# A list schedule that follows TensorE's column quarters, and a closing product on 128 rows

## The chip, the cores and the metric

The kernel runs on one core of a Trainium2 chip. The metric is device microseconds (us) of one execution, taken over several runs. The core's engines each take their instructions strictly in the order in which the program has them: PE (TensorE, matrix products into the accumulators of PSUM), DVE (VectorE), ACT (ScalarE), POOL (GpSimd), and SP, which here only issues DMAs. An engine whose next instruction must wait for another engine keeps everything behind it waiting too.

## The reference, cut to what matters

A recurrent attention over 768 steps, for 4 batches of 8 heads with 40 channels, and behind it two dense stages:

```python
for t in range(S):
    y[:, :, t] = np.einsum('bhd,bhde->bhe', rt, state)
    Sa = np.einsum('bhde,bhe->bhd', state, at)
    state_decay = state * wt[:, :, None, :] - np.einsum('bhd,bhe->bhde', Sa, bt)
    state = state_decay + np.einsum('bhd,bhe->bhde', vt, kt)
...
a = x @ w1
b = x @ w2
h = a * b @ w3
x = h @ w_out
...
h = x @ w_in
g = h * np.cos(h)
return g @ w_out
```

x has 3072 tokens of 320 channels; w1 and w2 are 320 x 1024, w_in is 320 x 2048.

## The kernel before

The 768 steps are cut into 24 chunks of 32 steps. All 32 pairs of batch and head go through a chunk together, as 16 pairs in two halves (hf 0 and 1). For each chunk the recurrence is turned into small dense products in fp32. In the order in which a chunk needs them they are called, by the functions that write them: **g** (`gstage`, 64x144, the chunk's own matrices), **mv** (32x64), **z** (40x64), **q** (32x72), **u** (32x72, on 32 rows), **y** (40x72) and **s** (40x40, the state for the next chunk). Each writes to a part of PSUM's partitions: a product with 32 output rows occupies one of TensorE's four column quarters, one with 40 or 64 rows two of them, one with 128 rows all four. In the profile every fp32 product is two records, so 16 products of y are "x32"; where the kernel's order is listed, it is one.

The products of four chunks (a group) need one triangular inverse, `tinv`, which DVE and POOL work out elementwise (dozens of operations on each). It ends with a transpose on DVE, `tfin`, which u of the group's first chunk waits for. There are six groups.

When two chunks are done, their output, 256 tokens, is one slab, and there are 12. `slab` loads it (`load_x`), `split_x` splits it into a high part `xh` (ACT) and a low part (POOL), each number being held as the sum of two of the faster format fp32r, and `ab` multiplies it by w1 and w2: eight steps f, and in each, for w1 and for w2, a sum of eight products 128x256. The third block of 64 channels lies twice in the 128 rows of `xh[:, 2]`, and the weight block `R` holds the high part of the weights in rows 0 to 63 and their low part in rows 64 to 127; so one product of 128 rows covers two terms. The eighth product, the sum's closing one, has the 64 rows `R[H0]` against `xr`, the low part of the third block. Each sum is then copied and multiplied (ACT, DVE) and stored (`pd`). `fold34` multiplies w3 by w_out beforehand (six products 128x320 for each of 32 units, "f,f" in the profile), `convert` and `weights_c` unpack weights on DVE, ACT and POOL.

After the last chunk come the second dense stage's products for all 12 slabs (`x2`, `hh`, `oo`: 3456 products, all in fp32r).

What sets the order: the kernel's functions do not issue instructions. They record them in `Program`, and its `emit` (line 256) orders them by a list schedule: it keeps a clock for each engine and always lets the engine that is free first take, among the instructions whose inputs are there, the one with the longest chain of work behind it (`far`). The lengths come from `length` and from tables (COST, HOP between engines, STEP of a product). A product's length is scaled by the share of columns that it occupies, as if narrow products always ran side by side. When PE's next product is of another form (32 rows or more, fp32 or fp32r: `mode`), SWITCH is added, unless a sum that has been started can go on. All instructions are issued at line 318, so the profile's rows are told apart by the tiles that they write and read: xs is the slab's split input (xh, xl, xr), w among the ab rows its weights, X and r the chunk's matrices, mid small work tiles, sh the tiles of g and of the inverse.

Of the kernel before, what the change touches and what calls it, by code (L numbers as in the profile page):

```python
# [10 lines left out]
F32 = mybir.dt.float32  # L11
F32R = mybir.dt.float32r
I32 = mybir.dt.int32
ALU = mybir.AluOpType
# [12 lines left out]
T2 = 256  # L27
# [102 lines left out]
class Program:  # L130
# [104 lines left out]
    def length(self, n):  # L235
# [16 lines left out]
    def mode(self, n):  # L252
        kw = self.calls[n][3]
        return kw["lhsT"].ap[0][1] <= 32, kw["rhs"].dtype

    def emit(self, tc, nc):
        self.link()
        N = len(self.calls)
        eng = [c[0] for c in self.calls]
        cost = [self.length(n) for n in range(N)]  # L260
        after = [[] for _ in range(N)]
        for n, d in enumerate(self.deps):
            for j in d:
                after[j].append(n)
        far = [0.0] * N
        hop = lambda n, m: self.HOP[eng[n]] if eng[m] != eng[n] else self.OWN[eng[n]]
        for n in reversed(range(N)):
            x = cost[n][1] + (self.ISSUE + self.BEGIN + self.END if eng[n] == "sync" else 0)
            far[n] = x + max([far[m] + hop(n, m) for m in after[n]], default=0)
# [6 lines left out]
        lanes, moved = deque([0.0] * self.LANES), 0.0  # L276
# [3 lines left out]
        for k in range(N):  # L280
# [4 lines left out]
            n = heapq.heappop(ready[e])[1]  # L285
            if e == "tensor":
# [1039 lines left out]
```

## Time and profile before

| what | us |
|---|---|
| runs | 1219.82, 1231.59, 1233.6 (median 1231.59) |
| the profiled execution, a run of its own | 1221.59 |
| its span, first to last instruction | 1219.8 |

The mean granted clock of TensorE was 0.944 in the profiled execution. Its parts, marked by the inverse's transposes and the last y: up to 108 us the first group is prepared; to 712 us run the 24 chunks, with most of the ab products between; to 808 us the last ab products, the last weights and the start of the second dense stage; to the end that stage alone.

A row of a timeline reads: start in us, length in us, engine, operation, tiles out<-in, rows*columns of the product, shape of the moving operand, and how many records follow each other. The length runs to the end of the last record, and ends of products are modelled; so what a piece of work takes from PE is read from its start to the start of the next row. A row of the groups has busy time, mean ns of one, and the engine's idle time before them. A row of the waits has the engine that waits, the one waited for, us in total, times, and the longest.

### The profile page before, as it was taken

The page shows a single profiled execution, that of the slowest core. Times are in us where ns is not written, and L with a number is a line of the kernel's source. Part 1 is how long each engine was busy: PE and PEld are TensorE (multiplying, and loading weights), DVE is VectorE, ACT ScalarE, POOL GpSimd, SP SyncE. Part 2 cuts the span into 40 slices and gives each one's busy share as a digit, 9 for nine tenths or more (in the row PEclk, how much of TensorE's full clock was granted, in tenths as well). Part 3 has the DMA queues.
Part 4 walks back from the last instruction along what each step waited for, and adds up shares of the span by engine and source line. Part 5 has one row for each costly group of instructions (what it writes and reads, how often), then busy time and mean ns, then how long its engine had stood idle before and what let it go on. Part 6 is the DMA issues. An engine that isn't in the chain of part 4 may idle for free. (4 is left out here: it accounts for less than half of the span.)

```text
span 1219.8 us, 34120 instructions
## 1 busy us (share of the span) xinstructions
PE 1052.4 (86%) x13536; PEld 956.4 (78%) x13536; DVE 842.2 (69%) x1776; ACT 679.3 (56%) x1750; POOL 600.4 (49%) x734
## 2 busy tenths in 40 slices
PE   2434798869987998999889977999999999999997
PEld 1324687768776877878778865899999999999997
DVE  9797779668968887896796674785455554545444
ACT  5865545754676578478545542455455544555443
POOL 8666336435444533563566673463455443454222
PEclk9975799889988999999899987999999999999999
DMA  6643544443454445444446553411101111011000
GB/s 177 185 117 93 140 119 123 126 137 115 129 157 131 114 141 158 127 134 114 137 136 209 150 169 106 124 39 47 46 12 46 44 38 46 22 37 46 9 4 23
DMA packets 142128, 122.73 MB, mean 101 GB/s; under 512 B 68240, under 2 KB 114832, under 8 KB 140432
## 3 DMA queue, kind: packets, MB, share of 16 engines
q1 hardware_dynamic: 141824, 120.50, 34.4%
q8 instruction: 106, 1.74, 0.6%
q14 instruction: 54, 0.44, 0.1%
q10 hardware_dynamic: 144, 0.06, 0.0%
HBM read 86.95 MB, written 29.62 MB: 96 GB/s over the span
## 5 line engine op out<-in xcount | busy, mean ns | idle before, releaser
L318 PE MATMUL bank<-xs,w 128*128 128x256 f32 (+1 forms) x1536 | 281.3, 316 | 29.9 <-ACT xs L318 22.0
L318 PEld LDWEIGHTS bank<-xs,w 128*128 128x128 f32 (+1 forms) x1536 | 221.3, 200 | 75.2 <-ACT xs L318 23.8
L318 POOL TENSOR_TENSOR w<-w,w 128x512 fp32r<-128x512 f32 x96 | 127.9, 1333 | 237.5 <-ACT w L318 147.4
L318 POOL TENSOR_SCALAR_AFFINE_SELECT X<-X 32x256 f32<-32x256 f32 (+1 forms) x144 | 98.6, 685 | 113.2 <-ACT X L318 92.1
L318 ACT COPY mid<-bank 128x256 f32<-128x256 f32 (+2 forms) x190 | 71.7, 394 | 144.9 <-PE bank L318 138.3
L318 ACT COPY X<-bank 32x128 f32<-32x128 f32 (+1 forms) x384 | 124.3, 324 | 41.8 <-PE bank L318 36.3
L318 DVE SCALAR_TENSOR_TENSOR w<-w,bank 128x512 f32<-128x512 int32 x96 | 65.8, 687 | 117.6 <-ACT w L318 106.0
L318 ACT COPY r<-bank 64x160 f32<-64x160 f32 (+2 forms) x408 | 113.4, 281 | 43.7 <-PE bank L318 38.7
L318 PE MATMUL bank<-X,r 104*40 104x72 f32 (+3 forms) x3072 | 124.2, 238 | 12.8 <-POOL X L318 7.1
L318 DVE TENSOR_TENSOR X<-bank,mid 40x128 f32<-40x128 f32 (+1 forms) x276 | 97.9, 355 | 51.0 <-PE bank L318 46.0
L318 PE MATMUL bank<-xs,r 128*128 128x256 f32 x576 | 130.5, 282 | 0.5 <-DVE xs L318 0.5
L318 PE MATMUL bank<-D,r 128*128 128x256 f32 x576 | 129.2, 282 | 1.8 <-DVE w L318 1.7
L318 PEld LDWEIGHTS bank<-X,r 104*40 104x40 f32 (+3 forms) x3072 | 104.5, 118 | 25.1 <-POOL X L318 8.6
L318 ACT CAST w<-w 128x512 fp32r<-128x512 f32 x120 | 73.6, 620 | 85.5 <-PE bank L318 70.5
L318 PE MATMUL bank<-mid 32*32 32x72 f32 (+2 forms) x3040 | 92.6, 233 | 26.6 <-ACT r L318 18.6
L318 PE MATMUL bank<-r,w 128*128 128x320 f32 x432 | 107.7, 311 | 0.6 <-ACT r L318 0.6
L318 PEld LDWEIGHTS bank<-mid 32*32 32x32 f32 (+2 forms) x3040 | 72.2, 126 | 42.7 <-ACT r L318 20.3
L318 PEld LDWEIGHTS bank<-D,r 128*128 128x128 f32 x576 | 99.2, 189 | 2.5 <-DVE w L318 2.2
L318 PEld LDWEIGHTS bank<-xs,r 128*128 128x128 f32 x576 | 99.9, 189 | 0.7 <-DVE xs L318 0.7
L318 DVE TENSOR_TENSOR sh<-sh,sh 128x110 f32<-128x110 f32 (+6 forms) x216 | 85.1, 394 | 2.4
L318 DVE SCALAR_TENSOR_TENSOR w<-w 128x512 f32<-128x512 int32 x96 | 84.6, 882 | 1.9
L318 PE MATMUL bank<-more,w 128*128 128x320 f32 x360 | 84.9, 310 | 0.0
(92 smaller groups left out, 2278.9 us busy)
## 6 DMA issues: line engine op xcount, KB each, us to landing
pd<-mid SPq DMA_DIRECT2D x96, 128.0 KB
f<-w3t SPq DMA_DIRECT2D x32, 256.0 KB
sh<-kb SPq DMA_DIRECT2D x48, 160.0 KB
sh<-wa SPq DMA_DIRECT2D x96, 80.0 KB
X<-pd SPq DMA_DIRECT2D x6, 1024.0 KB
w<-pd SPq DMA_DIRECT2D x6, 1024.0 KB
w34d<-f SPq DMA_DIRECT2D x32, 160.0 KB
r<-wo SPq DMA_DIRECT2D x16, 320.0 KB
```

The costliest lines, as they stand in the source:

```text
L318: getattr(getattr(nc, e), method)(*args, **kw)
```

## The change

Two things. First, the closing product of each ab sum has 128 rows: `split_x` makes a low part of all three blocks in one POOL operation of 128x768, in place of one of 128x512 and one of 64x256, and the sum ends with `R` against `xh[:, 2]` and `R` against `xl[:, 2]`. (The second of these adds the product of both low parts, which was left out.) No product with 64 rows is left.

Second, the list schedule. It keeps a time for each of the four column quarters (`array`); a product starts when its own quarters are free, and a product of another form when all are, plus SWITCH. If the first choice would have to wait for its quarters, `beside` takes another ready product of the same form whose quarters are free. `mode` tells 64 rows apart too. A sum that has been started still goes on ahead of a product of another form. HOP, and the lengths of DVE's and POOL's tensor_tensor and of DMAs, are longer, SWITCH shorter. The drawn variations (`rng`) are not used, since RUNS is 0.

```diff
-    STEP, DEEP = {True: 1.67, False: 0.457}, {True: 180, False: 185}
+    STEP, DEEP = {True: 1.67, False: 0.457}, 185
...
-        ("scalar", "copy"): (205, 0.72), ("scalar", "activation"): (200, 0.9), ("vector", "tensor_tensor"): (155, 1.1),
+        ("scalar", "copy"): (205, 0.72), ("scalar", "activation"): (200, 0.9), ("vector", "tensor_tensor"): (165, 1.25),
...
-        ("gpsimd", "tensor_tensor"): (330, 2.05), ("gpsimd", "affine_select"): (250, 1.2), ("gpsimd", "memset"): (110, 0.82),
+        ("gpsimd", "tensor_tensor"): (380, 2.3), ("gpsimd", "affine_select"): (250, 1.2), ("gpsimd", "memset"): (110, 0.82),
...
-    HOP = {"tensor": 95, "scalar": 65, "vector": 70, "gpsimd": 40, "sync": 60}
-    ISSUE, GAP, BEGIN, RATE, END, STORE, LANES, SWITCH, WAIT = 350, 55, 1350, 380, 1100, 600, 8, 120, 100
+    HOP = {"tensor": 140, "scalar": 110, "vector": 120, "gpsimd": 90, "sync": 60}
+    ISSUE, GAP, BEGIN, RATE, END, STORE, LANES, SWITCH, WAIT = 370, 60, 1350, 380, 1600, 600, 8, 90, 100
+    RUNS, LATE, VARY = 0, 500, {"vector": (0.9, 1.25), "gpsimd": (0.9, 1.4), "scalar": (0.95, 1.1)}
...
         if k == "matmul":
-            a = kw["rhs"]
-            w = min(x for x in (32, 64, 128) if x >= size(kw["lhsT"]))
-            step = 4 + self.STEP[a.dtype == F32] * size(a) * w / 128
-            return step, self.DEEP[a.dtype == F32] + step * 128 / w / 2 if a.dtype == F32 else self.DEEP[False] + step
+            f = kw["rhs"].dtype == F32
+            step = 2 + self.STEP[f] * size(kw["rhs"])
+            return step, self.DEEP + step / (2 if f else 1)
...
     def mode(self, n):
+
         kw = self.calls[n][3]
-        return kw["lhsT"].ap[0][1] <= 32, kw["rhs"].dtype
-
-    def emit(self, tc, nc):
-        self.link()
+        return kw["lhsT"].ap[0][1] <= 32, kw["lhsT"].ap[0][1] <= 64, kw["rhs"].dtype
+
+    def columns(self, n):
+
+        out = self.aps[n][0][0]
+        r = out.offset // math.prod(out.tensor.shape[1:])
+        return range(r // 32, (r + out.ap[0][1] + 31) // 32)
+
+    def beside(self, n, t, mode, array, ready, far):
+
+        if self.kinds[n] == mode and max(array[i] for i in self.quarters[n]) > t + 20:
+            x = min((x for x in ready if self.kinds[x[1]] == mode and max(array[i] for i in self.quarters[x[1]]) <= t + 5), default=None)
+            if x:
+                ready.remove(x)
+                ready.append((-far[n], n))
+                heapq.heapify(ready)
+                return x[1]
+        return n
+
...
-        lanes, moved = deque([0.0] * self.LANES), 0.0
+        lanes, moved, array = deque([0.0] * self.LANES), 0.0, [0.0] * 4
...
+            step, whole = cost[n]
             if e == "tensor":
-                if more is not None and not left[more] and self.mode(n) != mode and when[more] <= t + self.WAIT:
-                    if n != more:
-                        heapq.heappush(ready[e], (-far[n], n))
-                        n = more
-                        ready[e].remove((-far[n], n)) if (-far[n], n) in ready[e] else later[e].remove((when[n], n))
-                        heapq.heapify(ready[e])
-                        heapq.heapify(later[e])
-                        t = max(t, when[n])
+                if more is not None and more != n and not left[more] and self.kinds[n] != mode and when[more] <= t + self.WAIT:
+                    heapq.heappush(ready[e], (-far[n], n))
+                    n = more
+                    x = (-far[n], n)
+                    (ready if x in ready[e] else later)[e].remove(x if x in ready[e] else (when[n], n))
+                    heapq.heapify(ready[e])
+                    heapq.heapify(later[e])
+                    t = max(t, when[n])
+                    step, whole = cost[n]
+                else:
+                    n = self.beside(n, t, mode, array, ready[e], far)
+                    step, whole = cost[n]
                 more = self.sums.get(n)
-            step, whole = cost[n]
-            _, method, args, kw = self.calls[n]
-            if method == "matmul":
-                if self.mode(n) != mode:
-                    t += self.SWITCH
-                mode = self.mode(n)
-            if method == "dma_start":
+                if self.kinds[n] != mode:
+                    t = max(t, *array) + self.SWITCH
+                mode = self.kinds[n]
+                t = max(t, *(array[i] for i in self.quarters[n]))
+                for i in self.quarters[n]:
+                    array[i] = t + step
+                step = max(13, min(array) - t)
+            elif e == "sync":
                 t = max(t, lanes.popleft())
                 moved = max(moved, t + step + self.BEGIN) + whole
-                whole = moved + self.END + self.STORE * (kw["out"].space == DRAM) - t
+                whole = moved + self.END + self.STORE * (self.calls[n][3]["out"].space == DRAM) - t
+                if rng:
+                    whole += rng.expovariate(1 / self.LATE)
                 lanes.append(t + whole)
                 step += self.GAP
-            start[n] = (t, k)
+            elif rng:
...
+        runs = [self.run(far, cost, after, random.Random(k)) for k in range(self.RUNS)]
+        mean = self.run([-sum(x) for x in zip(*runs)] if runs else far, cost, after, None)
         with tc.manual_schedule():
-            for n in sorted(range(N), key=lambda n: start[n]):
+            for n in self.sorted(mean, after):
                 e, method, args, kw = self.calls[n]
                 getattr(getattr(nc, e), method)(*args, **kw)
+
...
-        xh, xl, xr = self.xh, self.xl, self.xr
+        xh, xl = self.xh, self.xl
         nc.scalar.copy(xh, xf)
-        nc.gpsimd.tensor_tensor(out=xl, in0=xf[:, 0:2], in1=xh[:, 0:2].bitcast(F32), op=ALU.subtract)
-        nc.gpsimd.tensor_tensor(out=xr, in0=xf[H0, 2], in1=xh[H0, 2].bitcast(F32), op=ALU.subtract)
-        return xh, xl, xr
+        nc.gpsimd.tensor_tensor(out=xl, in0=xf, in1=xh.bitcast(F32), op=ALU.subtract)
+        return xh, xl
...
-        xh, xl, xr = x
+        xh, xl = x
...
-            ops += [(R[:, w, fs], xh[:, 2])] + [(T[i][0][:, w, fs], xl[:, i]) for i in range(2)] + [(R[H0, w, fs], xr)]
+            ops += [(T[i][0][:, w, fs], xl[:, i]) for i in range(2)] + [(R[:, w, fs], xh[:, 2]), (R[:, w, fs], xl[:, 2])]
             for n, (l_, r_) in enumerate(ops):
                 nc.tensor.matmul(P[:, w], lhsT=l_, rhs=r_, start=(n == 0), stop=(n == len(ops) - 1))
...
-        self.xh, self.xl, self.xr = t(128, 3, T2), t(128, 2, T2), t(64, T2)
+        self.xh, self.xl = t(128, 3, T2), t(128, 3, T2)```

What moves, at two places. The first is PE in chunk 12, the first of the fourth group, from its first y product to its last ones before the next chunk. Names: X with r is y where it says 40x72, sh is g, r with X is s, mid 32x72 is u, xs is ab, and f with f is fold34. Before:

```order
L318 MATMUL bank<-X,r_77 40x72 x8
L318 MATMUL bank<-sh_63 64x144 x8
L318 MATMUL bank<-r_77,X 40x40 x16
L318 MATMUL bank<-mid 32x72 x16
L318 MATMUL bank<-X,r_77 40x72 x8
L318 MATMUL bank<-f_81,f_94 128x320
L318 MATMUL bank<-xs,w_88 128x256
L318 MATMUL bank<-f_81,f_94 128x320
```

The same place now:

```order
L357 MATMUL bank<-r_77,X 40x40 x16
L357 MATMUL bank<-X,r_77 40x72 x16
L357 MATMUL bank<-xs,w_88 128x256 x2
L357 MATMUL bank<-xs,w_90 128x256 x4
L357 MATMUL bank<-xs,w_88 128x256
L357 MATMUL bank<-xs,w_90 128x256 x3
L357 MATMUL bank<-sh_63 64x144 x8
L357 MATMUL bank<-mid 32x72 x16
```

The first half's 16 y products stood as two pieces of eight, each in one half of the columns, with g, s and u between; now they stand together, both halves by turns. Over the whole program, 228 of the y products followed one in the same columns directly; now it is 54. For q it is 76 and now 7, for s 27 and now 67. PE goes from fp32 into a stretch of fp32r products 158 times before and 136 times now; of the 192 closing products, 113 stood before an fp32 product, 57 inside a stretch ahead of a 128-row product, and 22 ahead of another closing one. Between fp32 products of different forms the order changes 118 times before, 141 times now. What stands in each chunk is otherwise nearly as it was: of the ab products, 168 stood behind the last y, now 180; ahead of y of chunk 12 stand 768 in both.

The second place is POOL around the split of the eleventh slab (xs<-mid,xs), with the recurrence's masks (AFFINE_SELECT on X) and the unpacking of weights (r, f, sh). Before:

```order
L318 TENSOR_TENSOR r_78<-r_73,r_78 128x256 x2
L318 AFFINE_SELECT X<-X 32x8x32 x2
L318 TENSOR_TENSOR xs<-mid,xs 128x512
L318 TENSOR_TENSOR xs<-mid,xs 64x256
L318 TENSOR_TENSOR f_95<-sh_64,f_95 128x640
L318 TENSOR_TENSOR r_78<-r_73,r_78 128x320
```

Now:

```order
L357 TENSOR_TENSOR r_78<-r_73,r_78 128x256
L357 AFFINE_SELECT X<-X 32x8x32 x2
L357 TENSOR_TENSOR r_78<-r_73,r_78 128x256
L357 TENSOR_TENSOR xs<-mid,xs 128x768
L357 TENSOR_TENSOR f_95<-sh_64,f_95 128x640
L357 AFFINE_SELECT X<-X 32x8x32
```

Two operations have become one, and its neighbours have changed places.

More of the change, by code (lines that the diff above doesn't have):

```diff
@@ L2 @@
 import math
+import random
 from collections import deque
@@ L253, in mode, with run @@
         kw = self.calls[n][3]
-        return kw["lhsT"].ap[0][1] <= 32, kw["rhs"].dtype
-    def emit(self, tc, nc):
-        self.link()
-        N = len(self.calls)
[L259 to L265, printed above, removed]
+        return kw["lhsT"].ap[0][1] <= 32, kw["lhsT"].ap[0][1] <= 64, kw["rhs"].dtype
[12 more added lines that the diff above has]
+        return n
+    def run(self, far, cost, after, rng):
+        N = len(self.calls)
+        eng = self.eng
         hop = lambda n, m: self.HOP[eng[n]] if eng[m] != eng[n] else self.OWN[eng[n]]
-        for n in reversed(range(N)):
-            x = cost[n][1] + (self.ISSUE + self.BEGIN + self.END if eng[n] == "sync" else 0)
-            far[n] = x + max([far[m] + hop(n, m) for m in after[n]], default=0)
         left = [len(d) for d in self.deps]
@@ L279, in emit @@
                 heapq.heappush(later[eng[n]], (0.0, n))
-        for k in range(N):
+        for _ in range(N):
             t, e = min((max(free[e], 0.0 if ready[e] else later[e][0][0]), e) for e in engines if ready[e] or later[e])
@@ L306, in emit @@
                 lanes.append(t + whole)
                 step += self.GAP
-            start[n] = (t, k)
+            elif rng:
+                step = whole = whole * rng.uniform(*self.VARY[e])
+            start[n] = t
             free[e], end = t + step, t + whole
@@ L314, in emit, with sorted @@
                     heapq.heappush(later[eng[m]], (when[m], m))
+        return start
+    def emit(self, tc, nc):
+        self.link()
+        N = len(self.calls)
+        eng = self.eng = [c[0] for c in self.calls]
+        cost = [self.length(n) for n in range(N)]
+        pe = [n for n in range(N) if eng[n] == "tensor"]
+        self.kinds, self.quarters = {n: self.mode(n) for n in pe}, {n: self.columns(n) for n in pe}
+        after = [[] for _ in range(N)]
+        for n, d in enumerate(self.deps):
+            for j in d:
+                after[j].append(n)
+        far = [0.0] * N
+        for n in reversed(range(N)):
+            x = cost[n][1] + (self.ISSUE + self.BEGIN + self.END if eng[n] == "sync" else 0)
+            far[n] = x + max([far[m] + (self.HOP[eng[n]] if eng[m] != eng[n] else self.OWN[eng[n]]) for m in after[n]], default=0)
+        runs = [self.run(far, cost, after, random.Random(k)) for k in range(self.RUNS)]
+        mean = self.run([-sum(x) for x in zip(*runs)] if runs else far, cost, after, None)
         with tc.manual_schedule():
-            for n in sorted(range(N), key=lambda n: start[n]):
+            for n in self.sorted(mean, after):
                 e, method, args, kw = self.calls[n]
                 getattr(getattr(nc, e), method)(*args, **kw)
+    def sorted(self, mean, after):
+        left = [len(d) for d in self.deps]
+        heap = [(mean[n], n) for n in range(len(left)) if not left[n]]
+        heapq.heapify(heap)
+        while heap:
+            _, n = heapq.heappop(heap)
+            yield n
+            for m in after[n]:
+                left[m] -= 1
+                if not left[m]:
+                    heapq.heappush(heap, (mean[m], m))
 class Kernel:
@@ L1016, in weights_a @@
         t = lambda p, *f: self.place("xs", p, *f, dt=F32R)
-        self.xh, self.xl, self.xr = t(128, 3, T2), t(128, 2, T2), t(64, T2)
+        self.xh, self.xl = t(128, 3, T2), t(128, 3, T2)
         self.turns["p"] = deque(self.place("mid", 128, T2) for _ in range(PB))
```

## The prediction, on record before the changed kernel ran

> **What bounds the kernel now.** I read the page first, then the busy time by stretches, then who waits for whom, and then PE's timeline at single products.
>
> ```profile
> span 1219.8 us, 34120 instructions
> PE 1052.4 (86%) x13536; PEld 956.4 (78%) x13536; DVE 842.2 (69%) x1776; ACT 679.3 (56%) x1750; POOL 600.4 (49%) x734
> ...
> PEclk9975799889988999999899987999999999999999
> ```
>
> PE is the busiest engine, but its clock is not always full, so the share must be read by stretches. In the next rows the columns are: stretch, its length, busy time (and records) of PE, PEld, DVE, ACT and POOL, granted clock, DMA share, GB/s. The bounds between 108 and 626.5 us are the starts of the inverse's transposes; 712 is the end of the last y.
>
> ```profile
> 108.00:211.10 103.10, 88.27 (x1492) 75.50 (x1484) 83.42 (x216) 53.01 (x159) 51.28 (x76) 0.85 0.45 123
> ...
> 325.30:438.90 113.60, 100.60 (x1742) 84.99 (x1741) 91.41 (x226) 71.14 (x217) 52.06 (x79) 0.94 0.48 135
> 438.90:547.50 108.60, 99.00 (x1750) 83.87 (x1748) 90.41 (x224) 75.17 (x234) 53.63 (x82) 0.97 0.50 141
> ...
> 626.50:712.00 85.50, 81.79 (x1524) 68.86 (x1524) 59.76 (x131) 43.75 (x120) 53.27 (x72) 1.00 0.61 179
> 712.00:808.00 96.00, 75.09 (x479) 67.46 (x477) 65.92 (x94) 36.15 (x77) 49.64 (x47) 0.88 0.38 120
> 808.00:1219.80 411.80, 404.55 (x3145) 403.97 (x3145) 207.03 (x300) 205.38 (x369) 172.99 (x127) 1.00 0.11 33
> ```
>
> The last stretch, a third of the time, is PE alone at full clock; its 3145 products are not touched by the change. In the chunks (108 to 712) a group takes some 110 us, PE is busy for nine tenths of it and DVE for eight tenths: two engines near their limit that pass work to each other. Who is late there:
>
> ```profile
> DVE X L318 <- PE bank L318: 46.0, 37, 4.7
> DVE mid L318 <- ACT mid L318: 25.4, 27, 2.9
> DVE D L318 <- PE bank L318: 10.1, 11, 2.4
> DVE sh L318 <- PE bank L318: 10.1, 9, 1.9
> ...
> PE bank L318 <- ACT r L318: 26.0, 15, 3.4
> PE bank L318 <- ACT xs L318: 14.3, 6, 4.4
> PE bank L318 <- POOL X L318: 7.1, 7, 1.8
> PE bank L318 <- DVE X L318: 5.1, 4, 3.1
> PE bank L318 <- DVE mid L318: 4.4, 7, 1.3
> ```
>
> In these 604 us DVE waited 46.0 + 10.1 + 10.1 = 66 us for PE itself, and PE waited 57 us for others (the five rows). So about half of the time in which one of the two holds up the other, 66 of 123, it is PE.
>
> **The closing product.** The groups name it, and the timeline gives its price.
>
> ```profile
> L318 PE MATMUL bank<-xs,w 128*128 128x256 f32 x1344 | 227.3, 308 | 29.9 <-ACT xs L318 22.0 <-DVE mid L318 7.4
> L318 PE MATMUL bank<-xs,w 64*128 64x256 f32 x192 | 68.6, 376 | 0.0
> ...
> 313.63 0.38 PE L318 MATMUL bank<-xs,w 64*128 64x256 f32 x1
> 313.94 0.31 PE L318 MATMUL bank<-mid 104*40 104x64 f32 x2
> 314.18 2.74 PE L318 MATMUL bank<-xs,w 128*128 128x256 f32 x16
> 316.85 0.31 PE L318 MATMUL bank<-mid 104*40 104x64 f32 x2
> ...
> 320.25 1.41 PE L318 MATMUL bank<-xs,w 128*128 128x256 f32 x8
> 321.59 1.14 PE L318 MATMUL bank<-f,f 128*128 128x320 f32 x6
> 322.66 0.59 PE L318 MATMUL bank<-sh 104*64 104x144 f32 x6
> ...
> 776.83 2.46 PE L318 MATMUL bank<-D,r 128*128 128x256 f32 x19
> 779.13 0.28 PE L318 MATMUL bank<-D,sh 128*128 128x256 f32 x1
> ```
>
> Start to start, 19 products of 128 rows take 2.30 us, 0.121 each. A closing product alone holds PE from 313.63 to 313.94: 0.31. The eight products from 320.25 to 321.59 take 1.34, and eight at 0.121 are 0.97. Some of the 0.37 between is the change from fp32 into fp32r and back: the six fold products from 321.59 to 322.66 take 1.07, of which six at 0.148 (from 0.121 by 320 columns instead of 256) are 0.89, so 0.18 is paid by any such stretch. That leaves 0.19 for a closing product at a stretch's end. The 16 products from 314.18 to 316.85, two sums one after the other, take 2.67: 1.33 more than eight, and eight at 0.121 are 0.97, so a closing product inside a stretch costs 0.36. By the counts of the order: 113 x 0.19 + 57 x 0.36 + 22 ahead of another closing one x 0.10 (an estimate between nothing and 0.19) = 21.5 + 20.5 + 2.2 = **44 us of PE** removed. Its place is taken by 192 products at 0.121, which are in the 0.97 already.
>
> **The split.** POOL loses one operation a slab.
>
> ```profile
> L318 POOL TENSOR_TENSOR xs<-mid,xs x24: 720/1280/2263, 144.8 to 727.2; 128x512 fp32r<-128x512 f32 x12, 64x256 fp32r<-64x256 f32 x12
> ...
> 728.10 5.88 DVE L318 TENSOR_SCALAR r<-r 128x256 int32<-128x256 int32 x1 [0.48 <-DMA r<-win]
> ...
> 736.86 0.28 DVE L318 TENSOR_SCALAR r<-r 128x256 int32<-128x256 int32 x1
> ...
> 725.79 2.42 POOL L318 TENSOR_TENSOR xs<-mid,xs 128x512 fp32r<-128x512 f32 x2
> ...
> 732.98 0.85 POOL L318 TENSOR_TENSOR r<-r,r 128x320 fp32r<-128x320 f32 x1
> ```
>
> The pair took 2.42 there. A 128x768 operation lies between half of that and some 2.4; I take 2.2. It saves POOL 12 x 0.2 = 2.4 us, which nobody waits for. Against it, the first xl product now waits for all three blocks, at most 0.7 us later a slab, 8 us for 12 slabs; four xh products (0.48 us) and other work stand ahead of it. I take 2 us, and keep 0 and 8 for the range.
>
> Here a page speaks against the change. The DVE operation at 728.10 took 5.88, where the same one at 736.86 took 0.28; it ended after POOL's operations up to 733.83 had. By the Trainium skill ("SBUF — State Buffer", "Who interferes with whom"), DVE and GpSimd share a port pair as an exclusive lock, and the loser waits for the whole instruction; one long operation would then hold DVE longer than the first of two, by up to the same 0.7 us a slab and 8 us in all. The trace goes further than the page: DVE did not get in between any of the POOL operations that stood back to back, the two of xs among them. By that row joining them costs nothing, and I add nothing.
>
> **The order.** Stretches of fp32r are entered 22 times less. Each entry costs the 0.18 from above and about 0.12 for the way in (the same drain, an estimate): 22 x 0.30 = 6.6 us. The y products:
>
> ```profile
> 458.72 1.19 PE L318 MATMUL bank<-X,r 128*40 128x72 f32 x16
> 459.84 0.41 PE L318 MATMUL bank<-f,f 128*128 128x320 f32 x1
> ...
> 707.75 1.20 PE L318 MATMUL bank<-X,r 104*40 104x72 f32 x32
> 708.88 0.39 PE L318 MATMUL bank<-xs,w 128*128 128x256 f32 x1
> ```
>
> Eight of them (x16) in one half of the columns take 1.12 us, and 16 by turns in both halves 1.13. So a product that follows one in its own columns costs about 0.065 more, and there are 228 - 54 = 174 fewer: 11.3 us. Against this, 40 more such successions among s (half as wide: 40 x 0.035 = 1.4 us) and 23 more changes of form among fp32 products (23 x 0.12 = 2.8 us). The 69 fewer of q I leave out; they lie beside other waits. Sum of the order: 6.6 + 11.3 - 1.4 - 2.8 = **14 us of PE**.
>
> The longer HOP and lengths have no row. They cost no engine time; they move which work is taken first. Their bounds are the waits: at best the 57 us of PE's waits go, at worst as much again comes. I take 0, since the order shows the same amount of ab work ahead of each chunk's y, to within some 20 products.
>
> **The sum.** 44 + 14 = 58 us of PE's time, less 2 for the split: 56. It counts where PE is late. After 712 us PE is the bound, but only 21 of the 192 closing products stand there: 4 us. For the rest, 52 us, I take the share 66/123 = 0.54 from the waits: 28. Together about 30 us. The profiled execution took 1221.59, which is 10 below the median of the runs (1231.59) and near the lowest of them (1219.82); I set the sum against 1227, the middle between the two: **1197 us**. If all 56 came through, against the profiled execution: 1166. If a quarter did: 1213.
>
> **Rivals.** (1) DVE and the hops are the bound in the chunks, and the time that PE saves becomes waiting: only the 4 us after 712 and the y products' shorter path (some 5 us) remain, and waits lower the clock. For it speaks that DVE is busy for 91.41 of 113.60 us; against it the 66 us that DVE waits for PE. Clock: in 108 to 211 us, where PE is busy for 88.27 of 103.10, it is 0.85, and 0.97 where it is busy for 99.00 of 108.60. If the saved 52 us turned into gaps and the clock of these 604 us fell by 0.01, that is 6 us back. It gives 1227 - 9 + 6, about 1224. The Trainium skill ("TensorE: Matmul & The Clock Gate", "HAM oscillation — how this bites in real kernels") tells the same of PE gaps above some 3.4 us, which halve the clock; the rows agree in direction only, since they show the mean.
>
> (2) Slower: the longer HOP makes the schedule put one more ab sum between the chain's dependent products in each chunk, and the recurrence's next product stands behind it in PE's queue. One sum of eight costs 8 x 0.121 = 0.97 us; at one a chunk and stage of q, u and y that is 24 x 3 x 0.97 = 70 us on the chain, less the 56 saved, and less nothing else: 1227 + 14 = 1241. It decides from 56 / (24 x 0.97) = 2.4 sums a chunk on. Against it: the ab work ahead of each y is unchanged in number.
>
> (3) The change does not do what it says: a closing product costs because it closes a sum, not for its 64 rows. Then the 44 us stay, and half of 14 - 2 gives 1221. The 19 products from 776.83 on belong to sums of eight that close with 128 rows, and take 0.121 each, so I give it no chance of its own; its time lies in rival 1's.
>
> (4) PE was the bound throughout, and the schedule's better lengths also remove waits: 1166 or a little less.
>
> **How the numbers follow.** Forecast (a quarter to four fifths of the sum kept, 1182 to 1213): 0.60. Rival 4 (1160 to 1182): 0.12. Rival 1 (1213 to 1235): 0.17. Rival 2 (over 1235): 0.11. What a measurement can tell from no change is about 1%, 12 us, so the bounds are 1219 and 1244. Faster: 0.60 + 0.12 + 0.04 from the fast end of rival 1 = 0.76. Slower: most of rival 2, 0.08. The same: 0.16. The range reaches from 1168 to 1232; it leaves out some 0.06 below and 0.13 above. The forecast's own range is 1182 to 1213.
>
> **What would show it.** In the changed kernel's profile the groups should have no 64*128 row, and 1536 xs,w products of 128*128 at a mean near 308 ns or below. Eight ab products between fp32 stretches should take some 1.15 us from start to start. DVE's waits for PE between the first transpose and the last y should fall from 66 to under 50 us, and the transposes should lie some 5 us closer together. The last stretch should still take 412 us. I am wrong if PE's waits in the chunks rise by as much as its work falls (rival 1), if q, u and y stand behind more ab work (rival 2), or if the time between the last y and the steady second stage (96 us) grows by over 10 us, for which I have no term.

## The result and the profile after

The changed kernel takes 1187.73 us (median of 4 runs, 1182.05 to 1193.11), the kernel before on the same chip 1225.75 (1219.82 to 1233.6): a ratio of 0.9685, interval 0.9597 to 0.9774, or 38 us less. Its profiled execution took 1190.81. The page, its first lines, the clock row and the costliest group:

```profile
span 1189.1 us, 34115 instructions
...
PE 1014.6 (85%) x13536; PEld 943.6 (79%) x13536; DVE 845.8 (71%) x1776; ACT 681.9 (57%) x1750; POOL 617.8 (52%) x722
...
PEclk8555898789998998898899989999999999999999
...
L357 PE MATMUL bank<-xs,w 128*128 128x256 f32 x1536 | 233.8, 302 | 21.0 <-ACT xs L357 8.1
```

PE is busy 37.8 us less than before, and no row with 64 rows is left. But the clock row has more small digits: the mean granted clock is 0.910, where it was 0.944. That is one execution each: the changed kernel's four ran at 0.908, 0.910, 0.940 and 0.956 and took 1193.11, 1190.81, 1182.05 and 1184.65 us. The stretches, with the columns as before (the bounds are again the transposes, two of the five groups are left out; 695.90 is the last y, 791.70 the start of the steady part):

```profile
105.70:209.60 103.90, 83.77 (x1576) 74.79 (x1576) 88.43 (x222) 62.23 (x187) 55.84 (x79) 0.89 0.48 134
318.90:430.80 111.90, 98.97 (x1750) 86.54 (x1745) 89.52 (x230) 72.58 (x221) 55.94 (x79) 0.94 0.51 144
430.80:545.10 114.30, 97.35 (x1711) 84.52 (x1710) 90.25 (x219) 72.41 (x223) 56.25 (x79) 0.90 0.47 131
617.50:695.90 78.40, 73.32 (x1533) 65.81 (x1529) 53.99 (x123) 43.09 (x118) 50.74 (x64) 0.96 0.64 187
695.90:791.70 95.80, 80.02 (x597) 77.65 (x597) 78.46 (x113) 46.68 (x98) 64.76 (x58) 0.93 0.42 134
791.70:1189.10 397.40, 391.07 (x3040) 390.81 (x3040) 204.62 (x289) 198.60 (x354) 167.15 (x122) 1.00 0.11 32
```

From the first transpose to the last y this execution takes 590.2 us, where it was 604.0; from the last y to the end 493.2, where it was 508.1. In the 590.2 us PE is busy for 509.6 and idle for 80.6; in the 604.0 before it was busy for 539.5 and idle for 64.5. So of 30 us that PE is busy less, 16 became idle time and 14 came through. The last row does the same work per product as before (391.07 / 3040 = 404.55 / 3145 = 0.129 us); there are fewer products in it, since in the 96 us ahead of it 597 got done instead of 479. The waits from 105.7 to 695.9 us (engine that waits, the one waited for, us, times, longest):

```profile
DVE X L357 <- PE bank L357: 43.0, 32, 6.5
...
PE bank L357 <- ACT r L357: 24.3, 14, 3.0
PE bank L357 <- POOL X L357: 23.5, 14, 3.9
...
PE bank L357 <- DVE mid L357: 11.4, 12, 2.3
...
DVE D L357 <- PE bank L357: 9.3, 8, 2.4
...
DVE sh L357 <- PE bank L357: 7.2, 6, 2.9
...
PE bank L357 <- DVE X L357: 2.1, 3, 1.5
...
PE bank L357 <- ACT xs L357: 1.9, 1, 1.9
```

DVE's waits for PE fell only from 66 to 59.5 us, and PE's own rose from 57 to 63: those for the high part of the slab's split (ACT xs) are nearly gone (14.3 to 1.9), those for the chain (POOL X, DVE mid) grew.

### The profile page after: what moved, and what is told of

Read it like the earlier page. It is cut to its first block, busy times and chain, and to the rows that moved or that the text cites. A ratio compares the mean times of both kernels' runs of the same rounds, so it can differ in the third digit from the quotient of the medians.

```text
span 1189.1 us, 34115 instructions
## 1 busy us (share of the span) xinstructions
PE 1014.6 (85%) x13536; PEld 943.6 (79%) x13536; DVE 845.8 (71%) x1776; ACT 681.9 (57%) x1750; POOL 617.8 (52%) x722
## 4 chain that ended last, share of the span: by engine, by line
PE 65%; DVE 10%; ACT 10%; DMA 5%; issue 4%; POOL 4%; SPq 1%; ACTq 0%; DVEq 0%; POOLq 0%
PE bank L357 65%; ACT r L357 4%; DVE sh L357 3%; ACT sh L357 3%; ACT X L357 2%; DVE r L357 2%; POOL X L357 2%; DVE f L357 2%; DMA X<-pd 1%; DVE w L357 1%; POOL r L357 1%; SPq L357 1%; DVE X L357 1%; DVE mid L357 1%; DMA mid<-yd 1%
## 5 line engine op out<-in xcount | busy, mean ns | idle before, releaser
L357 PE MATMUL bank<-xs,w 128*128 128x256 f32 x1536 | 233.8, 302 | 21.0 <-ACT xs L357 8.1
L357 POOL TENSOR_TENSOR w<-w,w 128x512 fp32r<-128x512 f32 x96 | 126.5, 1318 | 226.9 <-ACT w L357 174.1
L357 PEld LDWEIGHTS bank<-xs,w 128*128 128x128 f32 x1536 | 206.4, 202 | 37.4 <-DVE mid L357 9.2
L357 POOL TENSOR_SCALAR_AFFINE_SELECT X<-X 32x256 f32<-32x256 f32 (+1 forms) x144 | 102.1, 709 | 129.9 <-ACT X L357 103.2
L357 PE MATMUL bank<-X,r 104*32 104x72 f32 (+3 forms) x3072 | 131.0, 250 | 33.2 <-POOL X L357 30.5
L357 ACT COPY r<-bank 64x160 f32<-64x160 f32 (+2 forms) x408 | 114.6, 281 | 74.6 <-PE bank L357 68.9
L357 DVE SCALAR_TENSOR_TENSOR w<-w,bank 128x512 f32<-128x512 int32 x96 | 65.9, 687 | 120.4 <-ACT w L357 117.0
L357 ACT COPY X<-bank 32x288 f32<-32x288 f32 (+1 forms) x384 | 124.6, 325 | 43.5 <-PE bank L357 38.0
L357 PEld LDWEIGHTS bank<-X,r 104*32 104x32 f32 (+3 forms) x3072 | 106.8, 126 | 51.8 <-POOL X L357 33.6
L357 DVE TENSOR_TENSOR X<-bank,mid 40x128 f32<-40x128 f32 (+1 forms) x276 | 98.1, 355 | 48.5 <-PE bank L357 43.0
L357 PE MATMUL bank<-xs,r 128*128 128x256 f32 x576 | 129.4, 282 | 0.1
L357 PE MATMUL bank<-D,r 128*128 128x256 f32 x576 | 129.3, 282 | 0.0
L357 ACT COPY mid<-bank 128x256 f32<-128x256 f32 (+2 forms) x190 | 71.3, 394 | 94.7 <-PE bank L357 84.1
L357 ACT CAST w<-w 128x512 fp32r<-128x512 f32 x120 | 72.9, 620 | 83.1 <-PE bank L357 63.0
L357 PE MATMUL bank<-mid 32*32 32x72 f32 (+2 forms) x3040 | 88.3, 236 | 33.0 <-ACT r L357 19.7
L357 PEld LDWEIGHTS bank<-mid 32*32 32x32 f32 (+2 forms) x3040 | 71.0, 127 | 47.2 <-ACT r L357 22.3
L357 PE MATMUL bank<-r,w 128*128 128x320 f32 x432 | 104.2, 310 | 0.0
L357 PEld LDWEIGHTS bank<-xs,r 128*128 128x128 f32 x576 | 98.9, 189 | 0.4 <-DVE xs L357 0.3
L357 PEld LDWEIGHTS bank<-D,r 128*128 128x128 f32 x576 | 99.0, 189 | 0.1
L357 DVE TENSOR_TENSOR w<-bank,w 128x512 f32<-128x512 f32 x96 | 66.0, 688 | 39.5 <-ACT w L357 39.5
L357 ACT ACTIVATE w<-bank 128x512 int32<-128x512 f32 x96 | 57.2, 597 | 60.6 <-PE bank L357 60.6
L357 DVE SCALAR_TENSOR_TENSOR w<-w 128x512 f32<-128x512 int32 x96 | 89.8, 936 | 1.8
```

What stands on the lines that cost most here:

```text
L357: getattr(getattr(nc, e), method)(*args, **kw)
```

## The experiments

Twelve kernels, up to four of them on one chip. Since the kernel before differs by some us from chip to chip (medians 1223 to 1231), ratios to it are compared. Two ratios have to lie some 0.01, or 12 us, apart before they can be told from each other by their intervals. Kernels on the same chip can be compared directly; the letter names the chip where it was the same. "Half of ab" and "no corner" ran twice, the others four times. "Chunks" is the time from the first transpose to the last y in the profiled execution, "end" the time from there to the last instruction, "clock" the mean granted clock of that execution.

| kernel | chip | us | ratio, interval | chunks | end | clock |
|---|---|---|---|---|---|---|
| before | | 1225.75 | 1 | 604 | 508 | 0.944 |
| changed | | 1187.73 | 0.9685 (0.9597 to 0.9774) | 590 | 493 | 0.910 |
| closing product only | A | 1201.53 | 0.9821 (0.976 to 0.9883) | 588 | 502 | 0.923 |
| schedule only | A | 1210.76 | 0.9891 (0.9831 to 0.9951) | 610 | 498 | 0.933 |
| old lengths | A | 1206.32 | 0.9847 (0.978 to 0.9913) | 597 | 496 | 0.904 |
| HOP + 5 | A | 1187.44 | 0.9705 (0.965 to 0.976) | 583 | 493 | 0.957 |
| old HOP | B | 1198.28 | 0.9762 (0.9681 to 0.9843) | 592 | 496 | 0.934 |
| without `beside` | B | 1186.50 | 0.9661 (0.9595 to 0.9726) | 583 | 494 | 0.939 |
| half of ab | B | 1183.97 | 0.9636 (0.9527 to 0.9746) | 581 | 493 | 0.894 |
| no corner | B | 1173.16 | 0.9548 (0.944 to 0.9657) | 582 | 491 | 0.941 |
| old list, new lengths | C | 1184.93 | 0.9656 (0.9608 to 0.9705) | 582 | 495 | 0.957 |
| 384 more ab products | C | 1212.76 | 0.9876 (0.9812 to 0.9941) | 614 | 494 | 0.936 |
| longer HOP | C | 1166.72 | 0.9525 (0.946 to 0.959) | 568 | 490 | 0.954 |
| longest HOP | C | 1174.32 | 0.9584 (0.949 to 0.9678) | 575 | 492 | 0.920 |

**The parts alone.** The list and lengths of before, with only the closing product and the joined split (of the edit, the sum's line is shown):

```diff
-            ops += [(R[:, w, fs], xh[:, 2])] + [(T[i][0][:, w, fs], xl[:, i]) for i in range(2)] + [(R[H0, w, fs], xr)]
+            ops += [(T[i][0][:, w, fs], xl[:, i]) for i in range(2)] + [(R[:, w, fs], xh[:, 2]), (R[:, w, fs], xl[:, 2])]
```

> Schedule and lengths of before, only the closing product on 128 rows and the joined split. Theory A (the inverse and the chunks' latencies set the pace while inverses are being worked out, so that PE's saving counts only in the last eight chunks and after the last y): first to fifth transpose 439 us, within 8, as in both kernels so far; last y to the end 508 down to about 500; in all 1205 to 1215. Theory B (PE's saving counts everywhere at about half): 44 us of PE gone, so first to fifth transpose about 425, in all about 1203.

And the reverse, the changed list and lengths with the 64-row closing product (the same lines the other way round):

> The new schedule and lengths with the old closing product on 64 rows. Theory A: the schedule alone removes some 14 us of PE and a few waits, so 1210 to 1222, the rest of the gain coming from the closing product where no inverse runs. Theory B: 14 us at half, 1218. A third possibility, that the gain is the schedule's alone: 1188 to 1195, and then the run with the closing product alone is near 1226.

The closing product alone gives 22 us (1 - 0.9821, of 1225), the schedule alone 13. In the closing product's kernel first to fifth transpose takes 427.3 us and the whole 1201.5, near theory B's 425 and 1203, so PE's saving counts in the stretch with the inverses too. By the pages PE is busy for 1009.2 us in it and for 1052.5 with the schedule alone, where it was 1052.4: the closing product takes 43 us of PE's work away, the schedule nothing that shows. (The clock was 0.923 and 0.933, against 0.944, which makes the records longer in both.) The two ratios multiply to 0.9714, within the changed kernel's interval, so the parts add up: neither needs the other. That the gain is the schedule's alone, the third possibility, is out.

**How fine the grain is.** Every HOP 5 ns longer moves the order in many places, and should mean nothing:

```diff
-    HOP = {"tensor": 140, "scalar": 110, "vector": 120, "gpsimd": 90, "sync": 60}
+    HOP = {"tensor": 145, "scalar": 115, "vector": 125, "gpsimd": 95, "sync": 60}
```

> The changed kernel with every engine's HOP 5 ns longer, a change that means nothing by itself. It measures how much a mere reshuffle of the list moves the time: by theory A and B alike 1188, and the distance from it is the grain below which no difference between schedules says anything. I expect up to 8 us.

1187.44 against 1187.73: the total is steady. Inside it, the chunks took 583 us where the changed kernel's profile has 590, at a clock of 0.957 and not 0.910. So a stage of one execution can be read to some 7 us only, and the changed kernel's chunks are better taken as 583 to 590.

**The lengths.** First HOP, tensor_tensor and the DMAs' numbers back to the old ones, in the changed list (SWITCH stays at 90):

```diff
-        ("scalar", "copy"): (205, 0.72), ("scalar", "activation"): (200, 0.9), ("vector", "tensor_tensor"): (165, 1.25),
+        ("scalar", "copy"): (205, 0.72), ("scalar", "activation"): (200, 0.9), ("vector", "tensor_tensor"): (155, 1.1),
...
-        ("gpsimd", "tensor_tensor"): (380, 2.3), ("gpsimd", "affine_select"): (250, 1.2), ("gpsimd", "memset"): (110, 0.82),
+        ("gpsimd", "tensor_tensor"): (330, 2.05), ("gpsimd", "affine_select"): (250, 1.2), ("gpsimd", "memset"): (110, 0.82),
...
-    HOP = {"tensor": 140, "scalar": 110, "vector": 120, "gpsimd": 90, "sync": 60}
-    ISSUE, GAP, BEGIN, RATE, END, STORE, LANES, SWITCH, WAIT = 370, 60, 1350, 380, 1600, 600, 8, 90, 100
+    HOP = {"tensor": 95, "scalar": 65, "vector": 70, "gpsimd": 40, "sync": 60}
+    ISSUE, GAP, BEGIN, RATE, END, STORE, LANES, SWITCH, WAIT = 350, 55, 1350, 380, 1100, 600, 8, 90, 100
```

> The changed kernel with the old HOP, tensor_tensor lengths and DMA times; quarters, forms and closing product stay. If the longer lengths are worth something of their own: 1195 or more, with more waits of PE in the chunks. If they are worth nothing: 1188, within 8.

Then HOP's line alone:

> The changed kernel with the old HOP alone; tensor_tensor and DMA lengths stay new. With all lengths old the time was 1206. If it is HOP that counts: 1200 or more; if it is the lengths of tensor_tensor and DMAs: 1188, within 7.

Then the reverse, the list of before (its code, its SWITCH) with the new lengths and the 128-row closing product:

> The list schedule of before (no quarters, old forms, old share of columns in a product's length) with the closing product on 128 rows and the new HOP, tensor_tensor and DMA lengths. If the longer lengths carry the schedule's gain and the quarters nothing: 1188, within 7. If the quarters count beside them: 1195 to 1202, as with the closing product alone.

With the old lengths the ratio rises from 0.9685 to 0.9847, by 20 us. And on the list of before, the new lengths bring 0.9821 down to 0.9656, by 20 again. So the lengths are worth some 20 us on either list. With the old HOP alone the ratio is 0.9762, 9 us up, which the intervals do not set apart, and 1198 lies between the two forecasts; on its own chip this kernel took 1197.07 to 1201.57 us, and the one without `beside`, whose ratio is the changed kernel's, 1185.43 to 1189.26. So HOP's part is there, and is about half. With old lengths PE's idle time in the chunks is 76.0 us, against 80.6: the lengths do not gain by fewer waits of PE there. The old list with new lengths is as fast as the whole change (0.003 less), and with old lengths the old list is faster by as little (0.9821 against 0.9847): the new list gives nothing that can be measured.

**The quarters.** The changed kernel without the choice of a product beside the first:

```diff
-                    n = self.beside(n, t, mode, array, ready[e], far)
+                    pass
```

> The changed kernel without the choice of another product whose column quarters are free; the quarters' times, forms and lengths stay. The y products in their own columns come back, 174 x 0.065 = 11 us of PE. If half of that counts: 1193. If the choice is what gained in the chunks: 1195 or more. If it is worth nothing: 1188, within 7.

By the kernels' orders this brings y's successions in the same columns back from 54 to 148 (228 before), and q's from 7 to some 115. The time stays: 0.9661. That settles little by itself: 94 x 0.065 = 6 us of PE, and half of that is 3 us, less than two ratios can show. From its first transpose to its last y PE is busy for about the same time as in the changed kernel (509.6 us at clock 0.90, by the sum of its records over 105.7 to 695.9):

```profile
106.70:689.90 583.20, 507.10 (x9568) 450.46 (x9569) 464.03 (x1180) 361.11 (x1086) 317.44 (x444) 0.91 0.50 140
```

**Does PE's work still count?** Half of the ab products are left out (those of the low parts, four of each sum's eight, some 93 us of PE):

```diff
-                ops += [(h[:, w, fs], xh[:, i]), (l[:, w, fs], xh[:, i])]
-            ops += [(T[i][0][:, w, fs], xl[:, i]) for i in range(2)] + [(R[:, w, fs], xh[:, 2]), (R[:, w, fs], xl[:, 2])]
+                ops += [(h[:, w, fs], xh[:, i])]
+            ops += [(R[:, w, fs], xh[:, 2]), (R[:, w, fs], xl[:, 2])]
```

> Leaves out four of the eight products of each ab sum (the terms with the weights' and the input's low parts of the first two blocks): 768 products, 92 us of PE, about 51 of them between the first and the fifth transpose. Theory A (inverse and latency set the pace there): first to fifth transpose shorter by at most 15 us, 425 or more; after the fifth and behind the last y most of the rest comes through. Theory B (PE counts at about half everywhere): first to fifth transpose near 411, in all near 1140.

And the other way, each sum's last product is added three times (384 more products, 46 us of PE):

```diff
-            ops += [(T[i][0][:, w, fs], xl[:, i]) for i in range(2)] + [(R[:, w, fs], xh[:, 2]), (R[:, w, fs], xl[:, 2])]
+            ops += [(T[i][0][:, w, fs], xl[:, i]) for i in range(2)] + [(R[:, w, fs], xh[:, 2])] + [(R[:, w, fs], xl[:, 2])] * 3
```

> The changed kernel with two more products in each ab sum (the last one is added three times in place of once): 384 products, 46 us of PE, 28 of them between the first and the fifth transpose. If PE has slack in the chunks after the change, as the run with half of the ab products says: 1188 to 1196, the rise lying behind the last y, and less time at the half clock. If PE is the bound again as soon as work is added: 1210 or more. The two together give the point where PE stops counting.

Adding 46 us costs 1.9%, 23 us: a half, as with the closing product, and all of it in the chunks; the end stays at 494, though the text before the run put the rise there. Taking 93 us away gains 0.5%, 6 us, and the intervals overlap. First to fifth transpose takes 429.9 us in the lighter kernel, as theory A had it, but what A expected behind the fifth did not come either: from there to the last y 150.9 us (150.8 in the changed kernel), and 493 to the end. The stretch of the chunks in the lighter kernel:

```profile
106.50:687.30 580.80, 469.95 (x8900) 393.28 (x8891) 461.99 (x1168) 359.56 (x1082) 298.73 (x438) 0.84 0.49 138
```

and in the heavier one:

```profile
105.10:719.00 613.90, 548.30 (x9888) 484.25 (x9889) 479.62 (x1190) 364.05 (x1090) 306.65 (x445) 0.91 0.47 134
```

The lighter kernel's PE runs 649 records less than the changed one in the chunks, worth 649 x 0.121 = 79 us, but is busy only 40 us less, since its clock is 0.84 and each product is longer (its ab group has a mean of 345 ns, where it was 302). The rest stands in its waits:

```profile
DVE X L357 <- PE bank L357: 54.1, 37, 5.1
...
PE bank L357 <- ACT r L357: 25.9, 14, 3.4
PE bank L357 <- POOL X L357: 20.5, 17, 2.9
PE bank L357 <- DVE mid L357: 16.2, 16, 2.8
```

DVE waits for PE no less than in kernels with all of the work (54.1 for X, against 43.0 in the changed kernel and 52.5 with HOP + 5), though PE has less to do.

**Is it DVE, then?** The inverse's lower left block ("corner") is left at zero, which takes DVE and POOL operations out of each group (DVE 845.8 to 799.5 us, POOL 617.8 to 552.5, by the pages):

```diff
-        for f in diagonal, middle, corner:
+        g.memset(N[:, 0:16, 0:16], 0.0)
+        for f in diagonal, middle:
```

> Leaves out the last third of each inverse (its corner is set to zero): 12 operations of DVE and 17 of POOL a group, about 8 us on each engine. Theory A: each group 6 to 8 us shorter, first to fifth transpose 407 to 415, in all 1155 to 1165. Theory B: PE has as much to do as before, so first to fifth transpose 430 or more, in all 1178 or more.

The ratio falls by 1.4%, 15 us by the medians; the two intervals overlap, but on the same chip the two runs (1171.48, 1174.85) lie over 10 us below all four without `beside`. Of these, 9.5 us lie ahead of the first transpose, which came at 96.2 us, not 105.7. The chunks themselves:

```profile
96.20:678.70 582.50, 505.35 (x9587) 443.66 (x9586) 438.16 (x1122) 364.55 (x1098) 258.16 (x360) 0.91 0.50 141
```

582.5 us, as in the kernels that have the corner, with 30 us less of DVE and 51 less of POOL. But the parts of it moved. First to fifth transpose takes 416.7 us, where the changed kernel and those of the same total that have the corner (HOP + 5, without `beside`, old list with new lengths) take 427.7 to 439.4; from the fifth to the last y it takes 165.7, where they take 146.7 to 155.5. So the inverse's work does count while the next inverse is worked out, and what is saved there is lost again behind the fifth transpose; why was not tested. Neither theory named this: the total lies between A's and B's. Over the whole of the chunks, taking away PE's work shortens them as little as taking away DVE's and POOL's, though adding PE's lengthens them. What holds them at some 583 us is not shown.

**HOP further out.** Since HOP gained, the same step again, and then one of 75 to 80 ns:

```diff
-    HOP = {"tensor": 140, "scalar": 110, "vector": 120, "gpsimd": 90, "sync": 60}
+    HOP = {"tensor": 185, "scalar": 155, "vector": 170, "gpsimd": 140, "sync": 60}
```

> The changed kernel with HOP another 45 to 50 ns longer (185, 155, 170, 140). If the step from the old to the new HOP paid because the real gaps between engines are longer still, a further step pays too: 1178 to 1184. If the new values are about right: 1188, within 7; too long, 1195 or more.

> HOP lengthened once more, by 75 to 80 ns beyond the last step (tensor 260, scalar 230, vector 250, gpsimd 220), everything else as in the changed kernel. The steps so far: old HOP 1198, the change's 1188, 45 to 50 ns more 1167. Theory A (a longer HOP is slack: the schedule puts other work between two dependent instructions, and the true lag and its scatter are longer than what stands in the tables): the gain flattens, since the planned distance now is beyond the 263 to 363 ns that products take to reach their readers: 1158 to 1172, with PE's waits in the chunks lower still. Theory B (the lag was under-priced and is now over-priced: too much work of ab is put ahead of the chain): the time turns up again, 1175 to 1195, with the inverse's transposes further apart than the 83 us a group of the last step. Theory C (HOP's effect is the luck of one order among many): anywhere between 1165 and 1200, with no order in the waits.

(The 83 us in the last text is a slip: the longer HOP's transposes stand 417.2 / 4 = 104 us apart up to the fifth; the longest HOP's stand 417.5 / 4, the same.) The longer HOP takes another 1.6% off, 20 us, and beats both kernels: 1166.72. It is the one edit after the change that clearly shortens the chunks (the longest HOP's lie within 7 us of the others'):

```profile
105.10:672.60 567.50, 494.09 (x9560) 433.13 (x9560) 466.44 (x1178) 360.00 (x1081) 307.81 (x441) 0.94 0.51 143
```

The same products and the same work of DVE, in 15 to 23 us less. Against the changed kernel and HOP + 5 all of it lies between the first and the fifth transpose (417.2 us, where they take 439.4 and 432.8). The 15 are against HOP + 5, whose mean clock was about the same (0.957 and 0.954). Against that kernel PE is busy 9.3 us less (503.4 there) and idle 6.2 less (79.6 there); whether the order or the clock in the chunks (0.94 against 0.93) made its products shorter was not separated. The longest HOP gives 0.9584, not to be told from 0.9525 by the intervals: the gain has ended. Its 1174.32 lies between the ranges of theories A and B, and inside C's. PE's five waits from above sum to 58.3 us with the longer HOP and 49.2 with the longest, against 63.2; but they sum to 55.4 with the old list and new lengths and 60.5 with HOP + 5, so fewer waits do not go with the shorter time. That the work put between dependent instructions stands there as slack against lags longer than planned was only argued, and the luck of one order among many (C) is not ruled out, though a step of 5 ns moved the total by less than 1 us.

A reading against the slack: where a reader had been idle, it began 274 ns (DVE, after y, 30 cases), 288 (ACT, after u, 29) or 375 (ACT, after q, 21) after the last product's start, medians from the changed kernel's records. The changed kernel's tables allow 386 for each of them (185, half of 2 + 1.67 x 72, and HOP's 140), more than any of the three; with the old HOP they allowed 341. Why a distance beyond the true one helps stays open.

## Why the prediction was right, and where it was not

The total was right (1197 said, 1188 measured, 30 us of gain said, 38 measured), but partly by luck: two terms were missed in opposite directions. Of the 30, some 8 were for the order, which brought nothing measurable; the longer lengths stood at nothing and brought some 20.

**The closing product** held in its price. These are rows of PE's timeline of the changed kernel, an early stretch and one with two sums:

```profile
149.94 1.22 PE L357 MATMUL bank<-xs,w 128*128 128x256 f32 x8
151.09 0.32 PE L357 MATMUL bank<-X,r 128*40 128x72 f32 x2
151.34 1.21 PE L357 MATMUL bank<-xs,w 128*128 128x256 f32 x8
152.48 0.70 PE L357 MATMUL bank<-X,r 104*40 104x72 f32 x16
...
285.00 2.18 PE L357 MATMUL bank<-xs,w 128*128 128x256 f32 x16
287.11 0.46 PE L357 MATMUL bank<-sh 104*64 104x144 f32 x2
```

Eight products take 1.15 and 1.14 us from start to start (1.34 before, some 1.15 forecast), sixteen 2.11 (2.67 before): 0.19 and 0.56 less, where the sum had 0.19 and 0.19 + 0.36. Rival 3 is out. One step of the working rests on the wrong row. The sum at 320.25 is followed by fold products, which are fp32r too, so its 1.34 holds no way back into fp32, and its 0.37 is the price inside a stretch. The price at a stretch's end needs a sum that is followed by fp32, as this one of the kernel before:

```profile
149.42 1.41 PE L318 MATMUL bank<-xs,w 128*128 128x256 f32 x8
150.76 0.30 PE L318 MATMUL bank<-mid 104*32 104x64 f32 x2
```

It takes 1.34 as well, and here the 0.18 comes off: 0.19. So both prices stand. Of the 44 us of PE, the kernel with this part alone gained 22, and the share read from the waits, 0.54, gave 24.

**The share** is the step that could have failed next. It held on the way in (22 of 44) and on the way back (46 us added cost 23), but taking away twice that gave 6. The change stops just where the share ends; beyond it lies rival 1's place, where saved work becomes waits and a lower clock. How the share was read is weaker than its number: the 57 us are PE's waits for ACT, POOL and DVE together, only 9.5 of them for DVE, so they are no balance between PE and DVE, and DVE's waits for PE, forecast under 50, stayed at 59.5. That 66/123 comes near a half may be luck. The transposes came closer by (518.5 - 511.8) / 5 = 1.3 us a group, not 5; the kernels of the same total show up to 3.6.

**The order, 14 us of PE with half of it kept, failed.** The successions in the same columns did fall from 228 to 54, but the whole old list, which has most of them back, cost nothing, with the new lengths and with the old. Either comparison alone would still admit the 8 us forecast, at the edge of its interval, but both point the other way. Beside HOP + 5, at the same mean clock (0.93 in the chunks of both), PE in the chunks of the old list with new lengths is busy 5.1 us more (508.5 against 503.4) and idle 5.8 less (73.8 against 79.6): what the new list saves of PE's time there became waits. The 22 fewer entries into fp32r stretches were put under the wrong heading for the most part: by the orders there are 158 before, 139 with the closing product alone, 145 with the schedule alone and 136 in the changed kernel, so 19 of them come with the closing product. Their price had 0.12 us for the way in, for which no row was given; the y product that stands alone between two stretches takes 0.25 (151.09 to 151.34 above), where one among its kind takes 0.07 to 0.14, so the size is not far off. The price of 0.065 us for a succession came from two stretches of y; that it adds up over 174 places, and reaches the end, was not shown by any row, and by these runs it does not.

**The longer lengths, taken as 0, failed the other way: about 20 us.** I had reasoned that they cost no engine time and leave the amount of ab work ahead of each y unchanged. Both are true, and neither makes the term nothing: the same instructions in another order gave the 20 us. Which places of the order give them was not found. The bounds of 57 us to both sides held it. Rival 2, a longer HOP that slows the chain, is the reverse of what the longer HOPs showed.

**The end** was forecast to give 4 us and gave 15. The closing product's part was right (508 to 502). The other 8 come with either half of the schedule: 496 us with the new list and the old lengths, 495 with the old list and the new lengths. The last weights and the start of the second stage were packed better, as the 597 products in place of 479 say; which entry does it was not separated. "The last stretch still takes 412" failed as written, since it began earlier with fewer products.

**The split.** A POOL operation over 128x768 took 1.88 us (median of 12), not 2.2, and PE waited for it 3.7 us in all (two forecast). The reading that DVE did not get in between the two xs operations was wrong. In the records of the kernel before, DVE's operation from 726.17 to 727.62 us took 1.45, where the median of the 32 of its kind is 0.49; it ended 0.35 after the first xs operation (725.79 to 727.27), while the second was running. So DVE did get in there, and joining the two could cost it something. The Trainium skill ("SBUF — State Buffer", "Who interferes with whom") says that the one that comes second to the shared ports is blocked for the other's whole instruction. By that rule a longer POOL operation could hold DVE longer. That the closing part alone came out at 22 of 24 us leaves little room for it, but it was not measured by itself.

## What to carry to other kernels

Price an edit by a kernel that does it alone: two terms can cancel in a total that looks right. What share of an engine's work counts is measured by adding and taking away work that nothing depends on; waits read from one profile only suggest it, and a share that holds one way need not hold the other. In a list schedule, try the planned lags before the cost model's finer points: one row of numbers, longer than the lags that were measured, was worth more here than a model of the array.

## What was not expected of the hardware

**The clock follows the busy share of short windows, not long waits.** Half clock comes in multiples of 3.4 us. These are stretches of that length in the changed kernel, in which PE's busy time is the second number and the clock the third from the end:

```profile
360.90:364.30 3.40, 0.65 (x32) 0.49 (x32) 3.36 (x31) 2.81 (x12) 1.95 (x3) 1.00 0.76 214
364.30:371.10 6.80, 5.74 (x80) 5.32 (x84) 6.74 (x18) 2.87 (x7) 6.20 (x8) 0.50 0.53 160
...
401.90:405.30 3.40, 1.96 (x34) 1.49 (x30) 3.26 (x6) 3.25 (x11) 2.64 (x5) 1.00 0.39 116
405.30:408.70 3.40, 3.40 (x34) 3.21 (x35) 1.91 (x3) 2.71 (x7) 2.93 (x4) 0.50 0.64 160
...
412.10:415.50 3.40, 1.93 (x31) 1.44 (x30) 3.40 (x7) 0.69 (x3) 3.06 (x5) 1.00 0.53 125
415.50:418.90 3.40, 3.40 (x14) 2.79 (x15) 3.40 (x7) 0.00 (x0) 3.12 (x4) 0.50 0.44 138
```

```profile
405.19 2.14 PE L357 MATMUL bank<-sh 104*64 104x144 f32 x16 [1.44 <-ACT r L357]
```

PE was busy for 1.96 of 3.4 us, its one wait there was 1.44 us long, and the next window ran at half clock, which then lasted at least until a window was nearly full (3.07 us or more, in the changed kernel's chunks). In the chunks of the kernel before, the changed one and the one with half of ab, 45 windows at full clock were followed by one at half clock; PE was busy for 2.0 us or less in 44 of them. Of the 358 at full clock that were followed by another at full clock, 6 had as little.

The Trainium skill ("TensorE: Matmul & The Clock Gate", "HAM oscillation — how this bites in real kernels") puts the half clock down to PE gaps above some 3.4 us. Here the window's length agrees and that condition does not, as a wait of 1.44 us was enough.

So independent products seem to have a worth beside their work: they keep the windows full. Between the first and the fifth transpose the kernel with half of ab had half clock for 160 us, the changed one for 91. How much of the time that costs was not separated. The four executions of the changed kernel and the four of HOP + 5 suggest some us: the four at a mean clock of 0.908 to 0.915 took 1189.3 to 1193.11, the four at 0.939 to 0.957 took 1182.05 to 1185.59. The old list with new lengths does not show it (1185.28 at 0.918, 1183.72 to 1185.17 at 0.955 to 0.959).
